# Second layer's first product with seven products for eight

## The chip, the cores and the metric

One core of a Trainium2 chip runs the whole program. The metric is the device time of one execution in microseconds (us); three runs of the kernel before gave 948.76, 949.13 and 949.52, median 949.13. A profile of one more execution is read below. Its engines are TensorE (PE, with its weight loads as PEld), VectorE (DVE), ScalarE (ACT), GpSimd (POOL) and SyncE (SP), which here only issues DMAs.

## The reference

Attention with random features over 4 batches, 8 heads, 576 tokens each (2304 tokens in all), then two layers over the 2304 x 512 result:

```
x = attention(q, k, v, omega)          # 2304 x 512
h = x @ moe_w_in                       # 512 -> 2048
x = (h * cos(h)) @ moe_w_out           # 2048 -> 512
h = x @ moe2_w_in
x = (h * clip(h + 3, 0, 6) / 6) @ moe2_w_out
```

Weights are float64, the output is float32.

## The kernel before

Everything lives transposed: features on the 128 partitions, tokens along the free dimension. `xx` is an SBUF tile of 4 x 2304 columns that holds the layer's input, later its output, as four feature chunks. To reach more than the precision of one fp32r matmul, every operand is split into a rounded part and the rest (`rnd`, L262, and `sub`, L270), and each product is three matmuls (`passes`, L741): high with high, low weight with high, high weight with low.

Each layer is cut into 16 hidden blocks of 128 (`f`) and into token blocks of 512 (the last one has 256). A slot (`slot`, L815) is one `f` on one token block: 12 matmuls of the first product (4 feature chunks x 3, L829) into one PSUM bank (`at` or `pt` in turn), the nonlinearity on ACT and DVE (`nonlinear`, L689), its split into `gh` and `gl`, and 12 matmuls of the second product (4 output chunks x 3, L851), which add up over all `f` in four PSUM banks (`kv0`, `kv1`, `h`, `h`). Layer one runs in two halves of eight `f`: the first half stores its sums in DRAM (`yy`), the second (blocks of mode "add", L551) loads them (`yp`) and writes `xx`. Layer two (mode "full", L553) takes all 16 `f` per token block, so that a bank pair for `h` alternates and a slot's second product follows some slots behind its first.

Weights arrive as raw 64-bit words. `weight` (L577) turns half an `f` (512 columns) into one fp32 tile `wt`: one ACT and four DVE instructions (L601 to L621), then a high part on ACT and a low part on DVE or POOL into `wh[f]` and `wl[f]`. Layer two's weights overwrite layer one's, `f` by `f`, as those get free.

The order on every engine is written out ahead. `Plan.add` (L88) registers each task with a due time, the engines that could do it with a cost on each, the tasks it comes after, and a ring of buffers that it takes a place from; `Plan.order` (L92) plays the plan through with these costs, always giving a free engine the ready task with the lowest due time, and the instructions are issued in the order that this gives. Rings (L48) have a fixed number of places, taken in rotation; each place is a tile of its own. All DMAs are issued from SP, in that order. The framework adds the waits from the data that instructions touch.

Of the kernel before, what the change touches and what calls it, by code (L numbers as in the profile page):

```python
# [32 lines left out]

N_LATE = 8
# [12 lines left out]
W_MD = 8.02  # L47
RINGS = {  # L48
    "xT": 4, "nat": 4, "v": 4, "sq": 4, "mx": 4, "P": 6, "qt": 3, "xn": 2, "kvs": 4, "rd": 4,
    "at": 2, "pt": 2, "h": 2, "kv0": 1, "kv1": 1, "ws": 3, "wt": 3, "mxh": 4, "mxl": 4, "wk": 3, "gh": 2, "gl": 2, "yp": 3,  # L50
}
Y_BANKS = ["kv0", "kv1", "h", "h"]
# [23 lines left out]
class Task:  # L76
    def __init__(self, name, seq, key, engs, fn, after, alloc, use, late):
        self.name, self.seq, self.key, self.engs, self.fn = name, seq, key, engs, fn
        self.after, self.alloc, self.use, self.late = after, alloc, use, late


class Plan:
# [5 lines left out]
    def add(self, name, key, engs, fn, after=(), alloc=None, use=(), late=False):  # L88
        assert name not in self.tasks, name
        self.tasks[name] = Task(name, len(self.tasks), key + BIAS.get(kind_of(name), 0.0), engs, fn, list(after), alloc, list(use), late)  # L90

    def order(self):  # L92
# [11 lines left out]
        for t in tasks.values():  # L104
            deps = set(t.after) | set(t.use)
# [8 lines left out]
        rings = {r: [] for r in RINGS}  # L114
# [12 lines left out]
        def can(t, now):  # L127
            if ready_at[t.name] > now:
                return ready_at[t.name]
            if t.alloc:  # L130
                q = rings[t.alloc]
                k = len(q) - RINGS[t.alloc]
                if k >= 0:
                    r = released.get(q[k])
                    if r is None:
                        return None
                    if r > now:
                        return r
            return 0.0

# [3 lines left out]
        while len(done) < len(tasks):  # L144
# [6 lines left out]
            while again:  # L151
                again = False
                for e in engines:
# [31 lines left out]
                    if t.alloc:  # L185
                        rings[t.alloc].append(t.name)
# [7 lines left out]
                    for n in out.get(t.name, ()):  # L194
                        need[n.name] -= 1
                        lat = LAT[e] + (0.1 if "t" in n.engs and e != "t" else 0.0)
# [11 lines left out]
def attention_moe_moe2_kernel(  # L208
# [17 lines left out]
    wp = ctx.enter_context(tc.tile_pool(name="wp", bufs=1))  # L226
    xp = ctx.enter_context(tc.tile_pool(name="xp", bufs=1))
    sb = ctx.enter_context(tc.tile_pool(name="sb", bufs=1))
    dp = ctx.enter_context(tc.tile_pool(name="dp", bufs=1, space=bass.MemoryType.DRAM))
    hps = ctx.enter_context(tc.tile_pool(name="hps", bufs=1, space=PSUM))  # L230
    actx = ExitStack()
    ap = actx.enter_context(tc.tile_pool(name="ap", bufs=1))
# [5 lines left out]
    def tile_of(pool, name, ring, shape, dt=F32):  # L238
        buf[name] = pool.tile(shape, dt, tag=ring, name=ring, bufs=RINGS[ring])
        return buf[name]  # L240

    def bank(name, ring):
        return tile_of(hps, name, ring, [128, 512])

    xx = xp.tile([128, KC, NT], F32, name="xx")
    yy = dp.tile([KC, 128, NT], F32, name="yy")
    wh, wl = {}, {}
    for f in range(NW):
        wh[f] = wp.tile([128, 1024], F32R, name=f"wh{f}")
        wl[f] = wp.tile([128, 1024], F32R, name=f"wl{f}")  # L250

    def open_late():
        actx.close()
        late_p = ctx.enter_context(tc.tile_pool(name="late_p", bufs=1, reuse_waits="tile"))
        for f in range(NW, NF):
            wh[f] = late_p.tile([128, 1024], F32R, name=f"wh{f}")
            wl[f] = late_p.tile([128, 1024], F32R, name=f"wl{f}")
# [16 lines left out]
    omd = ap.tile([128, M], F32, name="omd")  # L274
    ident = ap.tile([128, 128], F32, name="ident")
    zero = ap.tile([128, 256], F32, name="zero")
    half = ap.tile([128, M], F32, name="half")
    junk = ap.tile([128, 1], F32, name="junk")

    def warm(e):  # L280
        nc.vector.memset(zero, 0.0)
        p = bank("warm", "h")
# [28 lines left out]
    def chunk(kind, c, k, exp_after, lead, pr, prev, on_pe=False):  # L311
# [4 lines left out]
        def load(e):  # L316
            t = tile_of(ap, X, "xT", [128, 512])
# [5 lines left out]
        if not on_pe:  # L323
            add(A, k - lead + 0.5, {"d": 0.74},
                lambda e: nc.sync.dma_start(out=tile_of(ap, A, "nat", [128, 512]), in_=(kn if isk else qn)[c]), [("nat",) + prev] if prev else [], alloc="nat")
        if isk and c == 0:
            add("omr", k - lead + 0.01, {"d": 0.3}, lambda e: nc.sync.dma_start(out=omd, in_=omT))
        if isk:
            def load_v(e):
                nc.sync.dma_start(out=tile_of(ap, V, "v", [128, H * (D + 1)]), in_=vn[c])  # L330
# [3 lines left out]
        def square(e):  # L334
            a = tile_of(ap, A, "nat", [128, 512]) if on_pe else buf[A]
# [6 lines left out]
        def sums(e):  # L342
            sq = tile_of(ap, SQ, "sq", [128, 8])
# [17 lines left out]
        add(P0, k - 0.2, {"t": 0.01}, lambda e: bank(P0, pr), before, alloc=pr, use=[X])  # L361

        def proj(e):
            bank(("pj", kind, c, 1), pr)
# [22 lines left out]
        for hf in range(2):  # L387
            def tops(e, hf=hf):
                pj = buf["pj", kind, c, hf].rearrange("p (h m) -> p h m", h=4)
                if hf == 0:  # L390
                    tile_of(ap, MX, "mx", [128, 24])
# [18 lines left out]
        for hf in range(2):  # L410
            E = ("e", kind, c, hf)

            def exps(e, hf=hf, E=E):
                pj, mx = buf["pj", kind, c, hf], buf[MX]
                p = tile_of(ap, E, "P", [128, 512])
# [8 lines left out]
        if isk:  # L424
            for hf in range(2):
                E = ("e", kind, c, hf)
                for b, r0, r1 in rows(c):
                    def kv(e, b=b, r0=r0, r1=r1, hf=hf, E=E, first=not kv_parts[b, hf]):
                        if first:
                            bank(("kv", b, hf), f"kv{hf}")  # L430
# [16 lines left out]
                    if c == last_chunk[b] and b == rows(c)[0][0]:  # L447
                        def fin(e, b=b, hf=hf):
                            if hf == 0:
                                tile_of(ap, ("kvs", b, 0), "kvs", [128, 2, 260])  # L450
# [6 lines left out]
        for hf in range(2):  # L457
            E, TP, QT, NUM, RD = ("e", kind, c, hf), ("tp", c, hf), ("qt", c, hf), ("num", c, hf), ("rd", c, hf)

            def trq(e, E=E, TP=TP):  # L460
                p = bank(TP, "pt")
# [4 lines left out]
            def qt(e, TP=TP, QT=QT):  # L466
                rnd(e, tile_of(ap, QT, "qt", [128, 512]), buf[TP])
# [4 lines left out]
            def num(e, QT=QT, NUM=NUM, hf=hf):  # L472
                p = bank(NUM, "pt")
# [11 lines left out]
            def eps(e, NUM=NUM, RD=RD):  # L485
                rd = tile_of(ap, RD, "rd", [128, 8])
# [6 lines left out]
            def norm(e, NUM=NUM, RD=RD, hf=hf):  # L493
                p = buf[NUM][:, :260].rearrange("p (h d) -> p h d", h=4)
                rd = buf[RD]
                if hf == 0:
                    tile_of(ap, ("xn", c, 0), "xn", [128, H, D])
# [10 lines left out]
        def xtr(e):  # L508
            xn = buf["xn", c, 0]
            p = bank(("xt", c), "pt")  # L510
# [40 lines left out]
    blocks += [dict(m=1, t0=t0, n=n, fs=range(NW, NF), mode="add") for t0, n in whole]  # L551
    n_m1 = len(blocks)
    blocks += [dict(m=2, t0=t0, n=n, fs=range(NF), mode="full") for t0, n in whole]  # L553

    def last_use(f):
        return max(bi for bi in range(n_m1) if f in blocks[bi]["fs"])

# [18 lines left out]

    def weight(src, m, f, hf):  # L577
# [8 lines left out]
        elif f < NW:  # L586
            k = blocks[n_add]["t"] + 10.0 + 9.0 * j
        else:
            k = slots[where[n_m1, f]][2] - 30.0
        cols = slice(512 * hf, 512 * hf + 512)  # L590

        def load(e):
            t = tile_of(sb, ("ws",) + W, "ws", [128, 512, 2], U32)
            nc.sync.dma_start(out=t.rearrange("p c w -> p (c w)"), in_=src[f, :, 1024 * hf:1024 * hf + 1024])

        gate = W_GATE.get(j) if m == 1 else None
        add(("ws",) + W, k - 8, {"d": 1.5}, load, [last_w[0]] if last_w[0] else [], alloc="ws")

        def mag(e):
            w = tile_of(sb, ("wt",) + W, "wt", [128, 512])  # L600
            nc.scalar.activation(out=w, in_=buf[("ws",) + W][:, :, 1].bitcast(F32), func=ACTF.Abs)  # L601
# [11 lines left out]
        def sign(e):  # L613
            u = buf[("wt",) + W].bitcast(U32)
            nc.vector.scalar_tensor_tensor(
                out=u, in0=buf[("ws",) + W][:, :, 1], scalar=SIGN_HI, in1=u, op0=ALU.bitwise_and, op1=ALU.bitwise_or
            )

        def low(e):
            u = buf[("wt",) + W].bitcast(U32)  # L620
            nc.vector.scalar_tensor_tensor(  # L621
                out=u, in0=buf[("ws",) + W][:, :, 0], scalar=29, in1=u, op0=ALU.logical_shift_right, op1=ALU.bitwise_or
# [14 lines left out]
        if m == 2:  # L637
            g = slot_of(last_use(f), f)
            after += [("in", g, KC - 1)] if hf == 0 else [out_name(g, KC - 1)]

        add(("wh",) + W, k, {"a": 0.62}, lambda e: rnd(e, wh[f][:, cols], buf[T_]), after, use=[T_], late=late)
        add(("wl",) + W, k, {"p": 1.4} if m == 1 and f < WL_P else {"p": 1.4, "v": 0.72},
            lambda e: sub(e, wl[f][:, cols], buf[T_], wh[f][:, cols].bitcast(F32)), [("wh",) + W], use=[T_], late=late)
# [8 lines left out]
    for m, src in ((1, w1), (2, w2)):  # L652
        for f in range(NF):
            for hf in range(2):
                weight(src, m, f, hf)
# [3 lines left out]
    def x_split(bi, i):  # L659
# [18 lines left out]
        def hi(e):  # L678
            rnd(e, view(tile_of(sb, ("xh", bi, i), "mxh", [128, 512], F32R)), src())

        def lo(e):
            sub(e, view(tile_of(sb, ("xl", bi, i), "mxl", [128, 512], F32R)), src(), view(buf["xh", bi, i]).bitcast(F32))
# [6 lines left out]
    def nonlinear(g, m, k, n, IN, sn_after):  # L689
# [7 lines left out]
        if m == 1:  # L697

            def u1(e):
                nc.vector.tensor_scalar(  # L700
                    out=tile_of(sb, WK, "wk", [128, 512])[:, :n], in0=hb(), scalar1=0.25, scalar2=MAGIC, op0=ALU.add, op1=ALU.add
# [17 lines left out]
        else:  # L719
            def relu(e):  # L720
                nc.scalar.activation(  # L721
                    out=tile_of(sb, WK, "wk", [128, 512])[:, :n], in_=hb(), func=ACTF.Relu, bias=three
# [9 lines left out]
        def g_hi(e):  # L732
            rnd(e, tile_of(sb, GH, "gh", [128, 512], F32R)[:, :n], buf[WK][:, :n])

        def g_lo(e):
            sub(e, tile_of(sb, GL, "gl", [128, 512], F32R)[:, :n], buf[WK][:, :n], buf[GH][:, :n].bitcast(F32))
# [4 lines left out]
    def passes(f, xh, xl):  # L741
        return (wh[f], xh), (wl[f], xh), (wh[f], xl)

    def pair_slot(g):
# [5 lines left out]
        for q in range(4):  # L750
            def m_in(e, q=q):
                if q == 0:
                    bank(("h", g), "h")
# [16 lines left out]
                alloc=None if q else "h", use=[(x, bi, q % 2) for x in ("xh", "xl")] + ([("h", g)] if q else []))  # L770
# [4 lines left out]
        for ec in range(KC):  # L775
            def m_out(e, ec=ec):
                y2 = ec // 2
                if first and ec % 2 == 0:
                    bank(("y", bi, ec), Y_BANKS[y2])
# [16 lines left out]
                alloc=Y_BANKS[ec // 2] if al else None, use=[("gh", g), ("gl", g)] + ([] if al else [("y", bi, ec - ec % 2)]))  # L796
# [213 lines left out]
```

## Time and profile before

| What | us |
|---|---|
| median of 3 runs | 949.13 |
| span of the profiled execution (first to last instruction) | 947.4 |
| around the span (median less span) | 1.7 |
| TensorE busy in the span | 941.4 |
| VectorE busy | 581.1 |
| ScalarE busy | 441.2 |
| GpSimd busy | 89.9 |

The profiled execution's own time is not listed apart from its span; the runs agree within 0.8 us, so the median stands for it, and 1.7 us lie around the span. Attention and the first pieces of layer one fill the span to about 240 us, layer one goes on to about 555, and layer two's matmuls run from 544.9 to the end. A matmul's "busy" time includes its way through the array, which overlaps the next one; its cost is the distance from one start to the next.

### The profile page before, as it was taken

How to read it: one execution, taken by the hardware profiler on the slowest of the kernel's cores; microseconds unless marked ns; L12 is line 12 of the kernel's file. 1: busy time of each engine (PE TensorE's matmuls, PEld its weight loads, DVE VectorE, ACT ScalarE, POOL GpSimd, SP SyncE). 2: the span in 40 equal slices, each digit the busy share in tenths (PEclk: the TensorE clock that was granted, in tenths of full speed). 3: DMA queues.
4: the chain of work that ended last, by engine and by line, in shares of the span. 5: the costliest groups of instructions: out<-in, count | busy, mean ns of one | idle time of the engine just before them, and what ended most of it. 6: DMA issues, size and time to landing. Idle time of an engine off the chain costs nothing.

```text
span 947.4 us, 16225 instructions
## 1 busy us (share of the span) xinstructions
PE 941.4 (99%) x6582; PEld 817.0 (86%) x6582; DVE 581.1 (61%) x1095; ACT 441.2 (47%) x897; POOL 89.9 (9%) x86
## 2 busy tenths in 40 slices
PE   9999999999999999999999999999999999999998
PEld 8889899999888898888888988888888888888898
DVE  6899887555888998989474888442223223322322
ACT  6888887766444464533232544332224223322332
POOL 3444331111100000000000000000000000000000
PEclk9999999999999999999999999999999999999999
DMA  8776333100323233323110123001001000100010
GB/s 282 234 233 214 110 126 122 56 1 24 112 90 114 87 111 112 111 75 107 52 45 1 51 95 111 1 2 45 0 1 45 1 1 1 45 1 1 1 45 24
DMA packets 29963, 68.37 MB, mean 72 GB/s; under 512 B 3136, under 2 KB 7232, under 8 KB 29888
## 3 DMA queue, kind: packets, MB, share of 16 engines
q1 hardware_dynamic: 29888, 67.33, 21.7%
q8 instruction: 52, 0.85, 0.4%
q14 instruction: 23, 0.19, 0.1%
HBM read 57.88 MB, written 9.44 MB: 71 GB/s over the span
## 4 chain that ended last, share of the span: by engine, by line
PE 98%; ACT 1%; DVE 1%; issue 0%
PE at L829 19%; PE pt L829 19%; PE kv L851 18%; PE h L851 18%; PE kv L786 5%; PE h L760 5%; PE at L367 3%; PE kv L434 2%; PE pt L477 2%; PE pt L464 2%; PE h L367 1%; PE kv L927 1%; PE pt L512 1%; PE h L376 1%; PE at L376 1%; PE h L284 0%
## 5 line engine op out<-in xcount | busy, mean ns | idle before, releaser
L264 ACT ACTIVATE gh<-wk 128x512 fp32r<-128x512 f32 (+1 forms) x160 | 94.2, 589 | 117.1 <-DVE wk L727 39.4
L271 DVE TENSOR_TENSOR gl<-wk,gh 128x512 fp32r<-128x512 f32 (+1 forms) x144 | 92.3, 641 | 64.6 <-ACT gh L264 63.2
L829 PE MATMUL at<-mxh,wl 128*128 128x512 f32 (+1 forms) x288 | 105.3, 366 | 0.0
L829 PE MATMUL at<-mxh,wh 128*128 128x512 f32 (+1 forms) x288 | 105.3, 366 | 0.0
L851 PE MATMUL kv<-gh,wl 128*128 128x512 f32 (+1 forms) x288 | 105.3, 366 | 0.0
L829 PE MATMUL pt<-mxh,wl 128*128 128x512 f32 (+1 forms) x288 | 105.3, 366 | 0.0
L829 PE MATMUL pt<-mxh,wh 128*128 128x512 f32 (+1 forms) x288 | 105.3, 366 | 0.0
L851 PE MATMUL kv<-gh,wh 128*128 128x512 f32 (+1 forms) x288 | 105.3, 365 | 0.0
L829 PE MATMUL at<-mxl,wh 128*128 128x512 f32 (+1 forms) x288 | 105.2, 365 | 0.0
L829 PE MATMUL pt<-mxl,wh 128*128 128x512 f32 (+1 forms) x288 | 105.2, 365 | 0.0
L851 PE MATMUL h<-gh,wl 128*128 128x512 f32 (+1 forms) x288 | 105.2, 365 | 0.0
L851 PE MATMUL kv<-gl,wh 128*128 128x512 f32 (+1 forms) x288 | 105.2, 365 | 0.0
L851 PE MATMUL h<-gl,wh 128*128 128x512 f32 (+1 forms) x288 | 105.2, 365 | 0.0
L851 PE MATMUL h<-gh,wh 128*128 128x512 f32 (+1 forms) x288 | 105.2, 365 | 0.0
L710 ACT ACTIVATE wk<-wk,halfpi 128x512 f32<-128x512 f32 (+1 forms) x80 | 54.2, 679 | 91.8 <-DVE wk L706 91.7
L727 DVE SCALAR_TENSOR_TENSOR wk<-wk,at 128x512 f32<-128x512 f32 (+1 forms) x40 | 25.4, 634 | 96.7 <-ACT wk L721 96.7
L727 DVE SCALAR_TENSOR_TENSOR wk<-wk,pt 128x512 f32<-128x512 f32 (+1 forms) x40 | 25.4, 634 | 90.1 <-ACT wk L721 89.9
L721 ACT ACTIVATE wk<-at,three 128x512 f32<-128x512 f32 (+1 forms) x40 | 25.9, 647 | 104.5 <-PE at L829 104.5
L266 POOL TENSOR_SCALAR mxh<-xx 128x512 fp32r<-128x512 f32 (+1 forms) x20 | 16.2, 813 | 610.8 <-PE pt L829 337.3
L721 ACT ACTIVATE wk<-pt,three 128x512 f32<-128x512 f32 (+1 forms) x40 | 25.9, 647 | 92.1 <-PE pt L829 91.5
L851 PEld LDWEIGHTS kv<-gh,wh 128*128 128x128 f32 x288 | 54.3, 189 | 8.9
L851 PEld LDWEIGHTS h<-gh,wh 128*128 128x128 f32 x288 | 54.4, 189 | 8.9
(110 smaller groups left out, 2033.6 us busy)
## 6 DMA issues: line engine op xcount, KB each, us to landing
ws<-w SPq DMA_DIRECT2D x64, 512.0 KB, 3.8
v<-vn SPq DMA_DIRECT2D x18, 260.0 KB, 4.0
xT<-qT SPq DMA_DIRECT2D x18, 256.0 KB, 2.7
xT<-kT SPq DMA_DIRECT2D x17, 256.0 KB, 3.8
yy<-yp SPq DMA_DIRECT2D x16, 256.0 KB, 2.1
yp<-yy SPq DMA_DIRECT2D x16, 256.0 KB, 4.1
nat<-qn SPq DMA_DIRECT2D x15, 256.0 KB, 4.4
yT<-xx SPq DMA_DIRECT2D x9, 256.0 KB, 2.7
```

The costliest lines, as they stand in the source:

```text
L264: nc.scalar.activation(out=o, in_=i, func=ACTF.Copy)
L271: (nc.gpsimd if e == "p" else nc.vector).tensor_tensor(out=o, in0=a, in1=b, op=ALU.subtract)
L367: nc.tensor.matmul(out=buf["pj", kind, c, o][:, 128 * i:128 * i + 128], lhsT=buf[X][64 * o:64 * o + 64, 128 * i:128 * i + 128], rhs=omd[64 ...
L376: nc.tensor.matmul(out=buf["pj", kind, c, o][:, 128 * i:128 * i + 128], lhsT=buf[A][64 * o:64 * o + 64, 128 * i:128 * i + 128], rhs=half[6 ...
L434: nc.tensor.matmul(out=p[j:j + 64, 65 * h:65 * h + 65], lhsT=buf[E][r0:r1, 128 * h + j:128 * h + j + 64], rhs=buf[V][r0:r1, 65 * (2 * h + ...
L710: nc.scalar.activation(out=r, in_=r, func=ACTF.Sin, scale=-TURN, bias=halfpi)
L721: nc.scalar.activation(out=tile_of(sb, WK, "wk", [128, 512])[:, :n], in_=hb(), func=ACTF.Relu, bias=three)
L727: nc.vector.scalar_tensor_tensor(out=w, in0=w, scalar=6.0, in1=hb(), op0=ALU.min, op1=ALU.mult)
L760: nc.tensor.matmul(out=o, lhsT=w[:, 128 * kc:128 * kc + 128], rhs=v, start=(kc == 0 and j == 0), stop=(kc == KC - 1 and j == 2), skip_grou ...
L786: nc.tensor.matmul(out=y, lhsT=w[:, o], rhs=v, start=(first and fi == 0 and j == 0 and ec % 2 == 0), stop=(last and fi == 1 and j == 2 and ...
L829: nc.tensor.matmul(out=buf["h", g][:, :n], lhsT=w[:, 128 * kc:128 * kc + 128], rhs=x, start=(kc == 0 and j == 0), stop=(kc == KC - 1 and j ...
L851: nc.tensor.matmul(out=buf["y", bi, ec][:, :n], lhsT=w[:, o], rhs=x, start=(first and j == 0), stop=(last and j == 2),)
```

## The change

Layer two is rewritten; attention and layer one keep their instructions.

- **First product.** Hidden blocks are taken in pairs (`j`, 8 of them) and tokens in passes of 768 (`p`, 3 of them), each pass seen as two halves of 384 columns. For a pair and a pass (a "quad" in the code, 24 of them) the 2 x 2 product over (two hidden blocks) x (two feature pairs) x (two token halves) is made with seven products, Strassen's scheme in Winograd's form. Each product is 6 matmuls of 384 columns (2 feature chunks x 3). ACT copies a PSUM bank into another bank at three places, so that later products add to an earlier sum; one bank is copied to SBUF and added on DVE.
- **Forms.** The sums of weights that the seven products need (`pair_forms`) and the sums of tokens (`forms`, seven per pass, each 2 x 768 columns, high and low) are made on DVE, ACT and POOL. The token forms of a pass are written to DRAM (`xd`) when first made and loaded again on later visits.
- **Order.** Four sweeps of two pairs go over the three passes, back and forth: 12 steps of two quads. The second product of a step comes in 8 units (12 matmuls of 384 columns, over two pairs, in one of two PSUM banks); its result is added into `xx` by DVE (in the first sweep written by ACT or DVE).
- **Places.** SBUF is now four large tiles (`R1`, `R2`, `F1`, `F2`) and every ring is a list of column ranges in them; the planner picks the place that gets free first, and for the rings in `TURNS` the next in turn. PSUM is eight fixed bank tiles.
- **Layer one.** Its last five blocks come in the order 0, 4, 1, 2, 3, and the loads of `yp` may start two slots earlier.

The diff, cut to its core:

```diff
+T_P = 31.1
+NS = 384
+NP = 2 * NS
+SWEEP = 2
 RINGS = {
-    "xT": 4, ... "at": 2, "pt": 2, "h": 2, "kv0": 1, "kv1": 1, "ws": 3, "wt": 3, "mxh": 4, ...
+    **stacked(R1, 0, ("w0", 2048, NG)),
+    **stacked(R2, 0, ("w1", 2048, NF - NG)),
...
+    "hb": spread(PS, 0, 1, 4) + spread(PS, 6, 1, 2),
+    "yb": spread(PS, 4, 1, 2),
+    "wf": spread(R1, 0, 3584, 2) + spread(R2, 0, 3584, 1),
+    "wo": spread(R1, 7168, 2048, 2) + spread(R2, 3584, 2048, 1),
+    "xf": spread(R1, 11264, 1536, 3) + spread(R2, 5632, 1536, 5),
+    "g2": spread(R1, 16384, 768, 8) + spread(R2, 13312, 768, 4),
...
+    "ta": spread(F1, XX + 1024, 768, 2),
+    "hs": spread(F1, XX + 2560, 384, 1) + spread(F1, XX + 5632, 384, 2),
+    "wk2": spread(F1, XX + 6400, 384, 3),
 }
-    blocks += [dict(m=1, t0=t0, n=n, fs=range(NW, NF), mode="add") for t0, n in whole]
+    blocks += [dict(m=1, t0=t0, n=n, fs=range(NW, NF), mode="add") for t0, n in whole[:1] + whole[4:] + whole[1:4]]
-    blocks += [dict(m=2, t0=t0, n=n, fs=range(NF), mode="full") for t0, n in whole]
+    ORDER = [0, 4, 1, 5, 6, 2, 3]
+    WITH = [(0, "b11"), (1, "b21"), (6, "b22"), (2, "t4"), (3, "t1"), (4, "t2"), (5, "t3")]
...
+        def forms(s, p):
...
+            if s:
+                for i, x in enumerate(names):
+                    def load(e, X=X, i=i):
+                        nc.sync.dma_start(out=tile_of(X, [128, 2 * NP]).bitcast(F32), in_=xd[p, i])
...
+            sums = {"t1": ("b12", "b11"), "t3": ("b22", "b12"), "t2": ("b22", "t1"), "t4": ("b21", "t2")}
...
+                add(X, kk + 0.3, {"a": 0.78, "p": 1.3}, hi, after + gate, alloc="xf", use=use, soft=behind(names.index(x)))
+                add(("xfl", p, x), kk + 0.4, {"v": 0.88, "p": 1.9}, lo, [X], use=use + [X])
...
+            product(0, A, True, first, "hb")
+            seed(Bk, A, 1.1, [A])
+            product(4, E, True, [A], "hb")
...
+            c11 = product(1, A, False, [Bk, E])
+            u2 = product(5, Bk, False, [c11])
+            seed(C, Bk, 7.4, [u2])
+            u3 = product(6, Bk, False, [C, u2])
+            seed(Dk, Bk, 9.6, [u3])
+            c12 = product(2, C, False, [u3])
+            c21 = product(3, Dk, False, [c12])
...
+                add(WK, k + dk, {"a": 0.5}, relu, [done], alloc="wk2", use=[h])
+                add(("gg",) + G[1:], k + dk + 0.5, {"v": 0.48}, gg, use=[WK, h])
+                add(G, k + dk + 1.0, {"a": 0.45}, ghi, [("gg",) + G[1:]], alloc="g2", use=[WK])
+                add(("gl2",) + G[1:], k + dk + 1.5, {"v": 0.5}, glo, use=[WK, G])
...
+                        for i in range(SWEEP):
+                            for r in range(2):
+                                for a, v in ((h, g[:, 0:NS]), (l, g[:, 0:NS]), (h, g[:, NS:2 * NS])):
+                                    nc.tensor.matmul(out=o, lhsT=a, rhs=v, start=q == 0, stop=q == 6 * SWEEP - 1)
```

`seed(to, frm, ...)` is an ACT copy of 384 columns from bank `frm` into bank `to`.

## Rows read from the trace of the kernel before

**Rows 1.** The page, parts 1 and 2: busy us; GB/s in 40 slices.

```profile
PE 941.4 (99%) x6582; PEld 817.0 (86%) x6582; DVE 581.1 (61%) x1095; ACT 441.2 (47%) x897; POOL 89.9 (9%) x86
...
GB/s 282 234 233 214 110 126 122 56 1 24 112 90 114 87 111 112 111 75 107 52 45 1 51 95 111 1 2 45 0 1 45 1 1 1 45 1 1 1 45 24
```

**Rows 2.** The page, part 4: the chain that ended last, by engine.

```profile
PE 98%; ACT 1%; DVE 1%; issue 0%
```

**Rows 3.** Windows: stretch, length, busy PE PEld DVE ACT POOL, clock, DMA.

```profile
0.00:150.00 150.00, 147.94 (x2152) 133.72 (x2153) 128.88 (x267) 122.02 (x334) 57.45 (x56) 1.00 0.60 198
150.00:545.00 395.00, 394.75 (x2477) 344.73 (x2477) 304.52 (x583) 191.98 (x352) 27.35 (x26) 1.00 0.23 73
...
600.00:943.50 343.50, 343.50 (x1697) 292.29 (x1696) 101.88 (x163) 102.01 (x170) 3.75 (x4) 1.00 0.04 13
```

**Rows 4.** Chain by time, two stretches: start, us, what, how many.

```profile
414.79 2.72 PE at L829 x12
...
901.94 1.44 PE pt L829 x12
```

**Rows 5.** Groups by form, PE, from 545: count, busy us, mean ns, idle.

```profile
L829 PE MATMUL at<-mxh,wh 128*128 128x512 f32 x128 | 49.8, 389 | 0.0
...
L829 PE MATMUL pt<-mxh,wh 128*128 128x256 f32 x32 | 9.1, 283 | 0.0
```

**Rows 6.** Timeline, DVE, 541.8 to 543: start, us, engine, line, instruction.

```profile
541.87 0.42 DVE L271 TENSOR_TENSOR gl<-wk,gh 128x256 fp32r<-128x256 f32 x1
542.21 0.69 DVE L271 TENSOR_TENSOR mxl<-xx,mxh 128x512 fp32r<-128x512 f32 x1
542.81 0.42 DVE L700 TENSOR_SCALAR wk<-pt 128x256 f32<-128x256 f32 x1
```

**Rows 7.** Groups by form, DVE, from 545: weights.

```profile
L621 DVE SCALAR_TENSOR_TENSOR wt<-ws,wt 128x512 uint32<-128x512 uint32 x12 | 8.2, 688 | 0.2
...
L609 DVE TENSOR_SCALAR wt<-wt 128x512 uint32<-128x512 uint32 x12 | 5.0, 423 | 0.2
```

**Rows 8.** Groups by form, ACT, from 545.

```profile
L264 ACT ACTIVATE gh<-wk 128x512 fp32r<-128x512 f32 x64 | 40.4, 631 | 48.4 <-DVE wk L727 38.9 <-PE h L851 8.2 <-DVE wt L621 1.2
L721 ACT ACTIVATE wk<-pt,three 128x512 f32<-128x512 f32 x32 | 22.1, 690 | 84.8 <-PE pt L829 84.7
...
L264 ACT ACTIVATE gh<-wk 128x256 fp32r<-128x256 f32 x18 | 7.5, 416 | 13.4 <-PE h L851 12.8 <-DVE wk L727 0.5
...
L868 ACT ACTIVATE xx<-kv 128x512 f32<-128x512 f32 x8 | 4.8, 598 | 0.6 <-PE kv L851 0.2
...
L868 ACT ACTIVATE xx<-kv 128x256 f32<-128x256 f32 x2 | 0.7, 384 | 1.5 <-PE kv L851 1.5
```

**Rows 9.** Timeline, 658 to 661; idle before and releaser in brackets.

```profile
658.09 0.39 PE L851 MATMUL kv<-gh,wh 128*128 128x512 f32 x1
658.29 0.69 ACT L721 ACTIVATE wk<-at,three 128x512 f32<-128x512 f32 x1 [3.36 <-PE at L829]
...
659.01 0.69 DVE L727 SCALAR_TENSOR_TENSOR wk<-wk,at 128x512 f32<-128x512 f32 x1 [3.36 <-ACT wk L721]
...
659.73 0.63 ACT L264 ACTIVATE gh<-wk 128x512 fp32r<-128x512 f32 x1 [0.75 <-DVE wk L727]
...
660.40 0.69 DVE L271 TENSOR_TENSOR gl<-wk,gh 128x512 fp32r<-128x512 f32 x1 [0.70 <-ACT gh L264]
```

**Rows 10.** DMA issues of the page: KB each, us to landing.

```profile
ws<-w SPq DMA_DIRECT2D x64, 512.0 KB, 3.8
```

**Rows 11.** Timeline, PE, 942 to the end: the last matmul.

```profile
943.42 0.28 PE L851 MATMUL h<-gl,wh 128*128 128x256 f32 x1
```

**Rows 12.** Groups by form, DVE, 0 to 150: weights, token splits.

```profile
L621 DVE SCALAR_TENSOR_TENSOR wt<-ws,wt 128x512 uint32<-128x512 uint32 x17 | 14.6, 856 | 0.1
...
L609 DVE TENSOR_SCALAR wt<-wt 128x512 uint32<-128x512 uint32 x19 | 13.0, 688 | 0.1
...
L271 DVE TENSOR_TENSOR mxl<-xx,mxh 128x512 fp32r<-128x512 f32 x6 | 5.4, 896 | 0.0
```

More of the change, by code (lines that the diff above doesn't have):

```diff
@@ L86, in __init__, with add @@
         self.tasks = {}
-    def add(self, name, key, engs, fn, after=(), alloc=None, use=(), late=False):
+    def add(self, name, key, engs, fn, after=(), alloc=None, use=(), late=False, soft=()):
         assert name not in self.tasks, name
-        self.tasks[name] = Task(name, len(self.tasks), key + BIAS.get(kind_of(name), 0.0), engs, fn, list(after), alloc, list(use), late)
+        self.tasks[name] = Task(name, len(self.tasks), key + BIAS.get(kind_of(name), 0.0), engs, fn, list(after), alloc, list(use), late, list(soft))
     def order(self):
@@ L104, in order @@
         for t in tasks.values():
-            deps = set(t.after) | set(t.use)
+            deps = set(t.after) | set(t.use) | set(t.soft)
             need[t.name] = len(deps)
@@ L130, in can, with slots_of, free_at, take @@
             if t.alloc:
[L131 to L138, printed above, removed]
-            return 0.0
+                r = min(free_at(x) for x in slots_of(t.alloc))[0]
+                if r == NEVER:
+                    return None
+                if r > now:
+                    return r
+            return 0.0
+        def slots_of(ring):
+            r = RINGS[ring]
+            return r if ring not in TURNS else [r[taken.get(ring, 0) % len(r)]]
+        def free_at(x):
+            space, lo, hi = x
+            at = 0.0
+            for o, l, h in live.get(space, ()):
+                if l < hi and lo < h:
+                    at = max(at, released.get(o, NEVER))
+            return at, lo, x
+        def take(t):
+            space, lo, hi = x = min(free_at(x) for x in slots_of(t.alloc))[2]
+            taken[t.alloc] = taken.get(t.alloc, 0) + 1
+            live[space] = [(o, l, h) for o, l, h in live.get(space, ()) if l >= hi or lo >= h] + [(t.name, lo, hi)]
+            self.slot[t.name] = x
         for t in tasks.values():
@@ L360, in chunk @@
         before = [("pj",) + prev + (1,)] if prev else []
-        add(P0, k - 0.2, {"t": 0.01}, lambda e: bank(P0, pr), before, alloc=pr, use=[X])
+        add(P0, k - 0.2, {"t": 0.01}, lambda e: bank(P0), before, alloc=pr, use=[X])
         def proj(e):
-            bank(("pj", kind, c, 1), pr)
+            bank(("pj", kind, c, 1))
             for i in range(4):
@@ L637, in weight @@
         if m == 2:
[L638 to L643, printed above, removed]
+            return
+        add(("wh",) + W, k, {"a": 0.62}, lambda e: rnd(e, wh(f)[:, cols], buf[T_]), after, alloc=None if hf else "w0" if f < NG else "w1",
+            use=[T_] + ([("wh", m, f, 0)] if hf else []), late=late)
+        add(("wl",) + W, k, {"p": 1.4} if f < WL_P else {"p": 1.4, "v": 0.72},
+            lambda e: sub(e, wl(f)[:, cols], buf[T_], wh(f)[:, cols].bitcast(F32)), [("wh",) + W], use=[T_, ("wh", m, f, 0)], late=late)
     def slot_of(bi, f):
@@ L650, in out_name @@
         return ("out", g, ec) if f != blocks[bi]["fs"][0] else ("y", bi, ec)
[L652 to L655, printed above, removed]
+    t_2[0] = t
+    for f in range(NF):
+        for hf in range(2):
+            weight(w1, 1, f, hf)
+    for j in range(NF // 2):
+        for hf in range(2):
+            for f in (2 * j, 2 * j + 1):
+                weight(w2, 2, f, hf)
     last_x = [None]
@@ L721, in relu @@
                 nc.scalar.activation(
-                    out=tile_of(sb, WK, "wk", [128, 512])[:, :n], in_=hb(), func=ACTF.Relu, bias=three
+                    out=tile_of(WK, [128, 512])[:, :n], in_=hb(), func=ACTF.Relu, bias=three
                 )
@@ L934, in filler @@
         if ("fill", ring) not in buf:
-            bank(("fill", ring), ring)
+            buf["fill", ring] = banks[RINGS[ring][0][1]]
         return lambda: nc.tensor.matmul(out=buf["fill", ring][:, 0:FILL], lhsT=zero[:, 0:128], rhs=zero[:, 0:FILL], start=True, stop=True)
```

409 lines of the change are left out of this document (335 added, 74 removed).

## The prediction

> **What bounds the kernel now.** I read the page first: TensorE is busy 941.4 of 947.4 us [rows 1], and the chain that ended last is 98% TensorE with nothing in "issue" [rows 2]. That figure alone is weak, because a matmul's busy time overlaps the next one's, so I went on to the windows [rows 3]: from 600 to 943.5 us, inside layer two, TensorE has no idle time at all, at full granted clock, while VectorE is busy 102 of 343.5 us, ScalarE 102 and GpSimd 4. Layer two is therefore bound by the number of matmuls times their spacing, and the other engines have two thirds of their time to give away. The chain by time gives the spacing [rows 4]: twelve matmuls of 512 columns take 2.72 us, 226.7 ns each; twelve of 256 columns take 1.44 us, 120.0 ns each. (The mean of 389 ns in the groups [rows 5] is latency; what is used from there is the count: 12 groups of 128, 1536 matmuls of 512 columns, and for the 256-token block 12 groups of 32, 384.)
>
> **What the change removes.** Before, layer two costs 1536 x 226.7 ns = 348.2 us and 384 x 120.0 ns = 46.1 us: 394.3 us. After, the first product has 24 quads x 7 products x 6 = 1008 matmuls of 384 columns instead of 1152 such, and the second 96 units x 12 = 1152, unchanged in columns. The trace holds no 384-column matmul. From both sides: 0.75 of the 512 price is 170.0 ns, 1.5 times the 256 price is 180.0 ns; midway between the two measured points on a line it is 173.3 ns, which I take, since both points lie about 13 ns above columns/2.4 GHz. Sum after: 2160 x 173.3 = 374.4 us. **Saved: 19.9 us** (ends 27.1 and 5.5). Weight loads change at every matmul in both versions and hide at 256 columns already.
>
> **What it adds beside TensorE.** Spacing on VectorE is 0.34 us for 256 columns and 0.60 for 512 [rows 6], so 0.47 for 384, 0.86 for 768, 1.12 for 1024. Per quad: two additions of banks, four `gg`, four low parts, 10 x 0.47 = 4.7 us, times 24 = 113. Additions into `xx` in sweeps two to four: 72 x 0.47 = 34. Token forms: 3 passes x (7 low parts + 4 sums) x 0.86 = 28. Weights: 32 halves x (2 x 0.42 + 2 x 0.69 = 2.2, [rows 7]) = 71, and per pair 2.1 for low parts of the forms, 1.4 for sums, 1.2 for the second weights, x 8 = 37. Together 283 us for 374 us of matmuls, 76%; some 37 us of it (two pairs, one pass) come before layer two starts. In the first sweep alone: 6 quads 28, two passes of forms 19, two pairs 27: 74 of 93 us. ScalarE: a bank copy of 384 is (598 + 384)/2 = 0.49 us, a rounding 0.52, a relu 0.58 (by the same slope) [rows 8]; 12 such per quad, 6.3 x 24 = 151, plus weights and forms of about 77: 228 of 374. Both fit beside TensorE; all of this costs nothing while it keeps its order, and shows as waits when it does not.
>
> **What it puts on the path.** Before, TensorE never waits in layer two because a bank's way to the next product takes 3.0 us (658.09 to 661.09, [rows 9]) and other slots' matmuls cover it. Now there are places with less cover.
> - *Bank copies.* The product `u3` needs bank C, which ScalarE copies after `u2`; what releases what in the timeline is 0.20 us from the last matmul to ScalarE [rows 9], 0.49 for the copy and some 0.06 back: 0.75 us. The first and third copy have a product of 6 x 0.173 = 1.04 us beside them; the second has nothing of its own quad and needs a unit (2.08 us) or a product of the next quad in between. The planner picks any ready task on TensorE, and in steps 2 to 12 units of the previous step are there: four per quad for one gap. Queued behind a copy on ScalarE are relus and roundings, and those hold banks. I take 2 us in all for copies that come late because ScalarE was in another instruction; ends 0 and 34 (second rival).
> - *The first step* has no units: the second quad's first products fill part of two bare gaps, 1.5 us (0 to 3).
> - *Token forms of passes two and three* can be made only as places of `xf` (eight for seven forms) get free, product by product. From the second quad of a step to the end of the next quad's products are 14.6 us of matmuls or more; VectorE needs 11 x 0.86 + 4.7 = 14.2 us in them. That only just fits: 2 us for both (0 to 10). Later visits load them from DRAM: 768 KB each, at most 7 in a 31 us step, 5.5 MB or 177 GB/s; the page shows slices at 282 GB/s [rows 1] and 512 KB landing in 3.8 us [rows 10], 5.7 us in proportion, against the 15 us between a place's release and its use. SP, which issues them, stands at each load until the product has released the place, and weight loads queue behind; they are due tens of us later. Cost 0 (0 to 6, in the range only).
> - *Seams of sweeps.* `wo` has three places for pairs; the second pair of a sweep gets its place when the last unit of the sweep before is through, two roundings and two low parts before the next unit. Products go on meanwhile: 1 us for three seams (0 to 6).
> - *The end.* The last units need the last product's relu, `gg`, rounding and low part: 0.20 + 0.58 + 0.56 + 0.52 + 0.56 + 0.1 = 2.5 us, with at most one unit of 2.08 before them: 1.5 us (0.4 to 2.5). From the last matmul (943.42, [rows 11]) to the end of the span are 4.0 us, a copy and a store; after it is an addition and a store, 0.
>
> Attention and layer one keep their instructions; the placement frees buffers by the same uses, and the reorder of five blocks moves nothing between engines: 0 (-2 to +2), since TensorE idles 2.3 us before 545 us in all [rows 3].
>
> **The sum.** 947.4 - 19.9 + (2 + 1.5 + 2 + 1 + 1.5 = 8.0) = 935.5 us of span. The profiled span lies 1.7 us under the median of the runs shown; with that, 937.2 us.
>
> **Rivals.**
> 1. *GpSimd slows VectorE.* The planner may give sums and low parts to GpSimd. In the first 150 us GpSimd is busy 57 us [rows 3], and there the same VectorE instructions take 856 instead of 688 ns, 688 instead of 423 [rows 7, 12], token splits 896 [rows 12] instead of 690 [rows 6]: 1.24 to 1.63 times. At 1.3 times, the first sweep's 74 us become 96, over the 93 of TensorE, and each later low part may come late: about 10 us more, 947 us. Against it: GpSimd needs twice VectorE's time by the planner's costs, so it gets a task only while VectorE is within a long one. The Trainium skill (SBUF — State Buffer, "Who interferes with whom") says that VectorE and GpSimd share a port pair as an exclusive lock: a VectorE instruction with two SBUF inputs, or in a two-port mode, blocks against a GpSimd instruction that reads SBUF, for its whole length. The trace agrees (the 1.24 to 1.63 above); by the rule the token sums would be the worst partners of GpSimd's low parts, and by it the time would be the 947 us just given.
> 2. *Bare bank copies (slower).* If no unit stands at the gap, because units were spent earlier in the step or their `g2` are late, each quad pays 0.75 us for the second copy, and each of three copies queues behind a ScalarE instruction (61% busy, half of 0.5 us left: 0.15, more behind one that itself waits, up to 0.6). With 0.75 + 0.65 per quad, 24 x 1.4 = 33.6 us: 947.4 - 19.9 + 33.6 + 6 + 1.7 = 969 us. It decides from 0.6 us per quad on, where 24 x 0.6 and the other 6 us have used up the saving. For it: seven products in a chain, six banks for five sums per quad. Against it: the plan puts any ready matmul in a gap, and the plan before kept TensorE idle for 2.3 us in 545.
> 3. *The saving is smaller than the count says.* If a 384-column matmul costs one and a half of the 256, 388.8 us remain: 947.4 - 5.5 + 8 + 1.7 = 951.6 us. For it only that the form is not in the trace; against it that the two prices differ by 13 ns of fixed cost.
> 4. *All gaps filled.* With 1.5 us at the end and 1 elsewhere: 947.4 - 19.9 + 2.5 + 1.7 = 931.7, down to 929 where the matmul costs 172 ns.
>
> **How the numbers follow.** Forecast 0.64, its own range 933 to 945; rival 1 0.11, rival 2 0.14, rival 3 0.03, rival 4 0.08. A measurement here can tell 0.2% (1.9 us) from no change: faster is below 947.2, slower above 951.0. The forecast and rival 4 are faster, rival 1 to two thirds, rival 2 is slower but for its lower edge; faster 0.79, same 0.07, slower 0.14. The range of 8 in 10 leaves out most of rival 2 and a little at the bottom: 929 to 950.
>
> **What would show it.** 384-column matmuls 173 ns apart; a step of 31.2 us of matmuls, and layer two's TensorE idle under 10 us, in pieces at the first two steps, the seams and the last 3 us before the final units. Wrong if TensorE waits on ScalarE's bank copies once per quad (rival 2), on VectorE's low parts with GpSimd busy (rival 1), or on loads of `xf`.

## The result: 937.84 us, where 937.2 was forecast

The changed kernel takes 937.84 us (median of 4 runs, 937.08 to 937.95); the kernel before took 949.06 beside it. The ratio is 0.9879, with a 95% interval of 0.9865 to 0.9892: faster, by 11.2 us. The number came out; the split behind it did not. Layer two gained more than forecast, and layer one lost time for which the forecast had no term.

The page of the changed kernel, part 1, answers to [rows 1] (busy us, share, instructions), and the windows answer to [rows 3] (stretch, length, busy PE PEld DVE ACT POOL, clock, DMA share, GB/s):

```profile
PE 928.4 (99%) x6822; PEld 857.9 (92%) x6822; DVE 681.2 (73%) x1295; ACT 500.8 (54%) x1048; POOL 88.8 (9%) x81
```

```profile
0.00:150.00 150.00, 147.42 (x2146) 133.21 (x2147) 128.83 (x264) 120.63 (x331) 60.12 (x56) 1.00 0.62 198
150.00:545.00 395.00, 394.75 (x2482) 341.65 (x2482) 288.61 (x541) 184.70 (x337) 22.72 (x21) 1.00 0.20 65
...
600.00:931.00 331.00, 331.00 (x1900) 331.00 (x1899) 215.26 (x413) 158.31 (x311) 5.94 (x4) 1.00 0.43 151
```

TensorE is as full as before. In the third line 1900 matmuls of 384 columns take 331 us, 174.2 ns each, with no idle time, though the busy share of VectorE is 2.2 times and that of ScalarE 1.6 times that of [rows 3]. Every wait of TensorE from 545 us to the end (engine, line, what it waited for: us in all, times, longest):

```profile
PE b L1186 <- DVE F L1220: 0.4, 1, 0.4
PE b L1186 <- ACT b L1198: 0.2, 1, 0.2
PE b L1186 <- DVE F L1238: 0.2, 1, 0.2
```

The first matmuls around each wait are further apart as well (283 to 287 ns for 174). Together the distances hold 1.9 us over their usual spacing in all of layer two, all of it before 577 us, in the first step. The end has no wait either: the last three matmuls follow at their usual distance. From the last one to the end of the span are 4.2 us, where it was 4.0 before [rows 11] (timeline: start, us, engine, line, instruction).

```profile
931.38 0.68 PE L1272 MATMUL b<-R 128*128 128x384 f32 x3
...
932.10 0.56 DVE L1289 SCALAR_TENSOR_TENSOR F<-b,F 128x384 f32<-128x384 f32 x1 [1.55 <-PE b L1272]
```

Layer two gained 16.0 us (17.9 of matmuls less 1.9 of waits, see the account below), but the span is only 11.4 us shorter. The chain by time (start, us, what, how many) shows where most of the rest went: into layer one, whose instructions are those of before. The last two lines are layer two's 384 columns.

```profile
302.59 2.72 PE b L939 x12
...
430.55 2.80 PE b L917 x12
433.35 2.80 PE b L939 x12
...
749.92 1.06 PE b L1186 x6
750.98 2.11 PE b L1272 x12
```

Twelve matmuls of 512 columns take 2.72 us in layer one's first half, as before it at 414.79 us [rows 4], and 2.80 in its second half. VectorE and ScalarE are less busy there than in [rows 3] (second line of each), and TensorE does not wait.

**The account of the span**, 947.4 to 936.0. Layer two's matmuls: 394.3 to 376.4 (2160 x 174.3), -17.9. Layer two's idle time: +1.9. Attention, until layer one's first slot: 238.96 to 239.66, +0.7. Layer one from there, with its last second products that run among layer two's first (36 of 256 columns before, 24 of 512 after): 544.88 + 4.3 - 238.96 = 310.2 before, 547.99 + 5.6 - 239.66 = 313.9 after, +3.7. Behind the last matmul: +0.2. Sum -11.4.

### The profile page after: what moved, and what is told of

It is laid out like the page before. It is cut to its first block, busy times and chain, and to the rows that moved or that the text cites. A ratio compares the mean times of both kernels' runs of the same rounds, so it can differ in the third digit from the quotient of the medians.

```text
span 936.0 us, 17221 instructions
## 1 busy us (share of the span) xinstructions
PE 928.4 (99%) x6822; PEld 857.9 (92%) x6822; DVE 681.2 (73%) x1295; ACT 500.8 (54%) x1048; POOL 88.8 (9%) x81
## 4 chain that ended last, share of the span: by engine, by line
PE 97%; ACT 1%; DMA 1%; DVE 1%; issue 0%; SPq 0%; ACTq 0%
PE b L1272 21%; PE b L1186 18%; PE b L917 17%; PE b L939 17%; PE b L874 5%; PE b L848 5%; PE b L446 4%; PE b L513 3%; PE b L556 2%; PE b L543 2%; PE b L455 2%; PE b L1323 1%; PE b L591 1%; DMA F<-kT 1%; ACT R L343 0%
## 5 line engine op out<-in xcount | busy, mean ns | idle before, releaser
L343 ACT ACTIVATE R<-F 128x512 fp32r<-128x512 f32 (+4 forms) x297 | 171.6, 599 | 113.8 <-DVE F L801 33.1
L350 DVE TENSOR_TENSOR R<-F,R 128x512 fp32r<-128x512 f32 (+4 forms) x273 | 179.3, 673 | 38.5 <-ACT R L343 32.5
L1272 PE MATMUL b<-R 128*128 128x384 f32 x684 | 141.4, 336 | 0.0
L1272 PEld LDWEIGHTS b<-R 128*128 128x128 f32 x684 | 120.9, 188 | 0.0
L1186 PE MATMUL b<-R,R 128*128 128x384 f32 x564 | 109.5, 336 | 0.7 <-DVE F L1220 0.4
L917 PE MATMUL b<-R,R 128*128 128x512 f32 (+1 forms) x480 | 106.5, 372 | 0.0
L939 PE MATMUL b<-R,R 128*128 128x512 f32 (+1 forms) x480 | 106.2, 372 | 0.0
L798 ACT ACTIVATE F<-F,halfpi 128x512 f32<-128x512 f32 (+1 forms) x80 | 54.3, 680 | 96.9 <-DVE F L794 96.8
L1272 PE MATMUL b<-R,R 128*128 128x384 f32 x468 | 102.3, 336 | 0.0
L1186 PEld LDWEIGHTS b<-R,R 128*128 128x128 f32 x564 | 98.6, 188 | 1.8 <-ACT b L1198 0.9
L939 PEld LDWEIGHTS b<-R,R 128*128 128x128 f32 x480 | 83.8, 188 | 17.4
L917 PEld LDWEIGHTS b<-R,R 128*128 128x128 f32 x480 | 82.8, 188 | 16.7
L350 POOL TENSOR_TENSOR R<-F,R 128x512 fp32r<-128x512 f32 (+1 forms) x36 | 47.6, 1322 | 494.0 <-ACT R L343 491.8
L1186 PE MATMUL b<-R 128*128 128x384 f32 x444 | 87.3, 337 | 0.2 <-DVE F L1238 0.2
L498 ACT ACTIVATE F<-b,F 128x128 f32<-128x128 f32 x288 | 81.1, 392 | 8.6 <-DVE F L483 6.3
L1272 PEld LDWEIGHTS b<-R,R 128*128 128x128 f32 x468 | 83.3, 188 | 0.0
L788 DVE TENSOR_SCALAR F<-b 128x512 f32<-128x512 f32 (+1 forms) x80 | 50.9, 636 | 43.5 <-PE b L917 26.7
L1186 PEld LDWEIGHTS b<-R 128*128 128x128 f32 x444 | 78.4, 188 | 0.6 <-DVE F L1238 0.5
L801 DVE TENSOR_TENSOR F<-b,F 128x512 f32<-128x512 f32 (+1 forms) x80 | 50.6, 633 | 21.1 <-ACT F L798 21.0
```

The costliest lines, as they stand in the source:

```text
L343: nc.scalar.activation(out=o, in_=i, func=ACTF.Copy)
L350: (nc.gpsimd if e == "p" else nc.vector).tensor_tensor(out=o, in0=a, in1=b, op=ALU.subtract)
L498: nc.scalar.activation(out=p[:, o], in_=pj[:, o], func=ACTF.Exp, scale=-1.0, bias=mx[:, b:b + 1])
L788: nc.vector.tensor_scalar(out=tile_of(WK, [128, 512])[:, :n], in0=hb(), scalar1=0.25, scalar2=MAGIC, op0=ALU.add, op1=ALU.add)
L798: nc.scalar.activation(out=r, in_=r, func=ACTF.Sin, scale=-TURN, bias=halfpi)
L801: nc.vector.tensor_tensor(out=buf[WK][:, :n], in0=hb(), in1=buf[WK][:, :n], op=ALU.mult)
```

## The experiments

**What differs in layer one's second half.** Its weights (`f` 8 to 15) are now in `R2`, which by the sizes of the tiles ahead of it starts 64 bytes further on modulo 128 than `R1`, where its tokens are. Before, all operands started at 64 modulo 128. My theory was placement: the spacing of matmuls depends on where weights and moving operand start relative to each other. The rivals were the new order of the last five blocks, and load from VectorE, ScalarE or DMA. Sorted by that phase, the 512-column matmuls of the changed kernel are 226.9 ns apart with equal phases and 233.3 with different ones; the 256-column ones 119.8 and 113.4.

*a1: only layer one's late weights move.*

```diff
-SIZES = {R1: 22528, R2: 16384, F1: 18112, F2: 16384}
+SIZES = {R1: 22528, R2: 16400, F1: 18096, F2: 16384}
-    "wf": spread(R1, 0, 3584, 2) + spread(R2, 0, 3584, 1),
+    "wf": spread(R1, 0, 3584, 2) + spread(R2, 16, 3584, 1),
...
```

(`wo`, `xf` and `g2` in `R2` 16 words further on as well, so that layer two stays where it was.)

> Layer one's weights of f 8 to 15 move 64 bytes down (from 64 to 0 modulo 128, where its tokens already are); layer two's tiles keep the class they had. Placement theory: the 768 matmuls of 512 columns of layer one's second half go from 233.3 to 226.9 ns (-4.9 us), the 192 of 256 columns from 113.4 to 119.8 (+1.2): time 934.1 us, 3.7 below the changed kernel. Rivals (the order of the last blocks, VectorE, ScalarE or DMA load beside them): no change, 937.8.

Measured: 934.93 us (5 runs, ratio to before 0.985, 0.9837 to 0.9863). The same place of the chain:

```profile
431.17 2.72 PE b L917 x12
433.89 2.72 PE b L939 x12
```

By the account above, layer one is 545.24 + 5.4 - 240.36 = 310.3 us, that of the kernel before. Placement carries the loss; the order of the blocks and the load were left as they were. The time fell by 2.9 us and not by 3.6, since in this profile attention ends 0.7 us later (240.36 for 239.66).

*a2: all of R2 moves.* `SIZES` has F1 at 18096 and nothing else changes.

> All of R2 moves 64 bytes down, so every matmul operand of the kernel starts at 0 modulo 128. Placement theory: layer one as in the run before (-3.7); layer two's products all at the 177.3 ns that this class showed instead of 175.9 on the mean (+1.4), units 174.5 for 174.4: 935.6 us. If the classes matter only at 512 and 256 columns: 934.1. Rivals without placement: 937.8.

Measured: 932.84 us (5 runs, 0.9828, 0.9816 to 0.9841), the fastest kernel here. Layer one is 310.3 us as in a1, and layer two gained too, against what I had read from the changed kernel's means by phase. From 600 us on:

```profile
600.00:928.00 328.00, 328.00 (x1894) 328.00 (x1893) 213.93 (x410) 157.12 (x309) 5.94 (x4) 1.00 0.42 151
```

That is 173.2 ns each, and all are 173 or 174 apart, where the changed kernel's lie between 168 and 185. A mean by the phase of one matmul misled me; a likely reason, not shown, is that in a mixed sequence the spacing belongs to the neighbours as much as to the matmul. From the first product to the end of the span: 386.0 us, 388.0 in the changed kernel.

*a3: the kernel before, with its late weights moved.*

```diff
+        late_p.tile([128, 16], F32, name="pad")
         for f in range(NW, NF):
             wh[f] = late_p.tile([128, 1024], F32R, name=f"wh{f}")
```

> The kernel before, with a pad of 64 bytes ahead of the weights of f 8 to 15 in both layers: these go from 64 to 0 modulo 128, tokens stay at 64. Placement theory: 1536 matmuls of 512 columns from 226.8 to 233.3 ns (+10.0), 384 of 256 columns from 119.9 to 113.4 (-2.5): 956.5 us, 7.5 above the kernel before. Rival (the changed kernel's order or load made its layer one longer): 949.1, no change.

Measured: 957.8 us (4 runs, 1.009, 1.0075 to 1.0104). The loss appears in the kernel before, with its order and its load:

```profile
441.54 1.40 PE kv L852 x6
442.94 1.40 PE h L852 x6
444.34 2.80 PE pt L830 x12
```

Six would be 1.36 us, half of the twelve of [rows 4]. Layer one is 314.1 us by the account, +3.9, and the rest is layer two's. The 512-column matmuls with different phases are 233.4 ns apart, the 256-column ones 115.7, not 113.4; hence 8.4 us and not 7.5.

*a4: layer two's weights at 64, its moving operands at 0 modulo 128.* Same edits as a1 with 16 and 32 words, and F1 at 18064, which brings `R2` to 0 modulo 256 while `R1` is at 128.

> Layer one with all operands at 0 modulo 128 (-3.7), layer two with all weights at 64 and all moving operands at 0. By the means of the changed kernel's classes: products 173.9 for 175.9 ns (1008: -2.0 us), units 175.4 for 174.4 (1152: +1.2): 933.3 us. If classes do nothing at 384 columns: 934.1. Rivals without placement: 937.8.

Measured: 939.92 us (4 runs, 0.9895, 0.9879 to 0.9911). A miss, and the most useful one: equal phases modulo 128 are not enough. Layer one's late weights and its tokens are now 128 bytes apart modulo 256, and those matmuls are 232.4 ns apart; in a1 and a2, where the two are 256 bytes apart modulo 512, they are 227 apart. The period is 256 bytes. By the account layer one is 314.3 us, 4.0 longer than in a1, which makes up most of the miss of 6.6 us; part of the rest is attention, which ends at 241.92 us in this profile.

*m1: TensorE alone.*

```
t = one SBUF tile; 8 phases of weights x 8 of the moving operand x (512, 384, 256 columns),
18 matmuls each: (h, xh), (l, xh), (h, xl) ..., nothing else running
```

> Nothing of the reference is computed: TensorE alone runs the sequence (high, high), (low, high), (high, low) at 512, 384 and 256 columns, with the start of the weights and of the moving operand each at the eight multiples of 32 bytes within 256; no other engine works beside it. Placement theory: with both at one phase 226.9, 173.3 and 119.9 ns; 64 bytes apart about 233 at 512 columns, 113 to 116 at 256, 173 to 177 at 384. Rival (the spacing came from what ran beside in the kernels): 226.9, 173.3 and 119.9 for every pair of phases.

Measured: one run of 624.46 us, with VectorE, ScalarE and GpSimd idle and DMA at rest in the stretch (windows):

```profile
100.00:200.00 100.00, 100.00 (x432) 80.81 (x431) 0.00 (x0) 0.00 (x0) 1.00 0.00 0
```

The median distance by phase of the moving operand less that of the weights, from the records of the trace (within each 18, without the first three distances):

```
bytes      0    32    64    96   128   160   192   224
512 cols 227.0 234.0 229.0 232.0 231.5 234.0 233.0 232.0
384 cols 173.0 173.0 173.0 176.0 175.0 173.0 174.0 174.0
256 cols 120.0 118.0 118.0 119.5 119.0 117.0 117.0 117.0
```

At 512 columns the effect is TensorE's own: the eight pairs of phases with the same difference modulo 256 lie within 1.4 ns of each other (means; the first group of the run left aside), which bears out the period. At 256 the change of sign is there, but the medians show only 3 ns of the 6.4 of the changed kernel. Its 113.4 ns (moving operand 64 bytes behind the weights, 192 in the table) appears in two of the eight pairs of that column, where the distances settle at 113 to 114 ns; the other six average 117.7. So at 256 columns the difference alone does not decide; what else does is open.

**What fills the gaps of the first product.** The next three kernels start from a2, whose even spacing lets a few us be read.

*b1: eight products for seven.*

```diff
-                    for kc in range(2):
+                    for kc in (0, 1, 0, 1) if i == 3 else (0, 1):
...
```

> On the kernel with all operands at one phase (932.84 us), the seventh product of each quad is made twice, so that eight are paid for (its bank holds a wrong sum). If layer two is the count of matmuls times their spacing: 24 x 6 x 173.3 ns = +25.0 us, 957.8 us. If waits in the chain of products set a part of the end, the extra matmuls fill them and the rise is smaller: with the 8 us of idle time of the forecast, +17, 949.8.

Measured: 955.38 us (4 runs, 1.0066, 1.005 to 1.0081), 22.5 over a2. Layer two by the profiles is 23.2 longer: 25.0 of matmuls, less some 1.7 of the first step's waits, which the extra product covers (its waits from 545 us on come to nothing that the view lists). The saving is the count of matmuls; without it, the second layer's new form is slower than the old (955.38 us, where the kernel before took 949.88 beside it).

*b2: units only between quads.*

```diff
+            m = n // 2
+            for t, u in ((m - 1, 3),) if n % 2 else ((m - 2, 7),):
+                if t >= 0:
+                    first = first + [("y2",) + tour[t] + (u,)]
...
+                        + [("sp", n0 + SWEEP + c, 3)]
```

> On the same kernel, the units of the second product run only between quads (four after each quad of the next step), so that no unit can stand at the second bank copy of a quad. Second rival of the forecast: 22 quads that had units x 0.75 us = +16.5, 949.3 us; with copies that queue behind other ScalarE work 1.4 each, +31, 963.6. If other matmuls than units cover the copies: 932.8 to 934.

Measured: 953.01 us (5 runs, 1.0041, 1.0027 to 1.0055), 20.2 over a2, slower than the kernel before. The waits from 545 us on, and one such place in the timeline:

```profile
PE b L1186 <- ACT b L1198: 14.8, 23, 1.0
```

```profile
834.38 0.86 PE L1186 MATMUL b<-R,R 128*128 128x384 f32 x4
...
834.99 0.66 ACT L686 ACTIVATE F<-F 128x512 f32<-128x512 f32 x1
835.55 0.48 ACT L1198 ACTIVATE b<-b 128x384 f32<-128x384 f32 x1
...
836.09 0.96 PE L1186 MATMUL b<-R,R 128*128 128x384 f32 x4 [0.85 <-ACT b L1198]
```

One copy per quad is bare. Of the 23, 16 cost 0.73 us at the next matmul and 0.10 in the one behind it; five cost 1.0 to 1.1 us at the next matmul, among them the place shown, where ScalarE was still in another instruction (L686). In the changed kernel the same copy lies beside a unit:

```profile
749.76 1.22 PE L1186 MATMUL b<-R,R 128*128 128x384 f32 x6
...
750.82 0.69 PE L1272 MATMUL b<-R,R 128*128 128x384 f32 x3
...
751.02 0.47 ACT L1198 ACTIVATE b<-b 128x384 f32<-128x384 f32 x1 [1.44 <-PE b L1186]
...
751.35 1.74 PE L1272 MATMUL b<-R 128*128 128x384 f32 x9
...
752.93 1.22 PE L1186 MATMUL b<-R 128*128 128x384 f32 x6
```

The product that the copy waits for is followed by the unit at 750.82, the copy ends at 751.49, and the product that needs it starts at 752.93, behind a unit (12 matmuls of L1272). By the order on TensorE at least one unit stands there in each of the last 21 quads, and a product of the next quad in the first three, ahead of the first units.

*c1: GpSimd beside layer two.*

```diff
+                    z = held((R1, 15872, 16384), [128, 512])
+                    sub("p", z, z.bitcast(F32), z.bitcast(F32))
...
+                add(("gp", m, i), start(m) + 2 * i, {"p": 1.75}, load, [("ba", m)] + ...)
```

> The kernel with all operands at one phase (932.84 us), and beside layer two eight GpSimd subtractions of 512 columns per quad (192 in all, on words that nothing else uses, about 1.7 us each, so that GpSimd is busy nearly throughout). First rival of the forecast: VectorE's instructions last 1.24 to 1.63 times as long; in the first sweep VectorE is busy 80.5 of 93 us, at 1.3 times 105, so TensorE waits about 12 us there, and the time is 943 to 945. If VectorE's spare time takes it: 933 to 935.

Measured: 1015.76 us (4 runs, 1.0696, 1.0679 to 1.0712), 82.9 over a2: a miss by far. Layer one took 13.6 us of it and layer two 69.2. GpSimd waits for nothing in these and ran ahead: 53 of 192 fell into layer one, the rest filled 545 to 735 us, at 1.3 us each. The window there, and VectorE's groups in it (count, busy us, mean ns, idle):

```profile
545.00:735.00 190.00, 141.29 (x653) 131.26 (x652) 177.40 (x166) 78.58 (x148) 179.19 (x139) 0.85 0.29 107
```

```profile
L350 DVE TENSOR_TENSOR R<-F,R 128x384 fp32r<-128x384 f32 x28 | 33.7, 1227 | 0.6 <-ACT R L343 0.6
...
L1238 DVE SCALAR_TENSOR_TENSOR F<-F 128x384 f32<-128x384 f32 x14 | 16.8, 1218 | 0.0
...
L1238 DVE SCALAR_TENSOR_TENSOR F<-F,b 128x384 f32<-128x384 f32 x14 | 7.6, 541 | 0.0
```

The changed kernel in the stretch from 548 to 735 us:

```profile
L350 DVE TENSOR_TENSOR R<-F,R 128x384 fp32r<-128x384 f32 x49 | 27.2, 575 | 2.4 <-ACT R L343 2.1
L1238 DVE SCALAR_TENSOR_TENSOR F<-F,b 128x384 f32<-128x384 f32 x25 | 13.8, 550 | 6.6 <-ACT F L1235 6.3
...
L1238 DVE SCALAR_TENSOR_TENSOR F<-F 128x384 f32<-128x384 f32 x24 | 13.2, 556 | 1.6 <-ACT F L1235 1.5
```

Factors of 2.1 and 2.2 for the forms with both inputs in SBUF, VectorE full, TensorE waiting 49 of 190 us at a mean granted clock of 0.85. The form of L1238 with one input in PSUM (`b`) kept its time: 541 ns for 550. TensorE's largest waits end at ScalarE's bank copies (27.8 us in 7), whose engine in turn waits for VectorE (most for L706, 24.9 us in 5):

```profile
PE b L1186 <- ACT b L1198: 27.8, 7, 7.2
```

That is the rule of the Trainium skill that the prediction named (SBUF — State Buffer, "Who interferes with whom"): only an instruction with two SBUF inputs, or in a two-port mode, is blocked. The trace shows the first half; that `TENSOR_SCALAR` of 512 columns with its one input in SBUF (L690) also went from 423 to 1094 ns would fit the second, but in which mode it ran is not shown.

*b3: layer one's last blocks back in order.*

```diff
-    ... for t0, n in whole[:1] + whole[4:] + whole[1:4]]
+    ... for t0, n in whole]
```

> The same kernel with layer one's last five blocks back in the order 0 to 4. If the order was a part of what layer one's second half lost or gained: a change of 0.5 us or more. If placement was all of it: layer one unchanged and the time 932.8, unless layer two's first step waits for the tokens of pass one (its products then start on blocks that were finished last): up to +3.

Measured: 946.81 us (10 runs, 942.99 to 948.96; 0.9966, 0.9952 to 0.998), 14.0 over a2 and more than either expectation. In this order part of the output is wrong, and why was not looked into; so the time is not that of a working kernel, and only waits and spacing are read here. From 545 to 600 us:

```profile
PE b L1186 <- DVE F L801: 4.8, 1, 4.8
PE b L1186 <- DVE F L1238: 2.8, 1, 2.8
```

```profile
554.37 0.42 DVE L801 TENSOR_TENSOR F<-b,F 128x256 f32<-128x256 f32 x1
...
554.84 1.97 PE L1186 MATMUL b<-R 128*128 128x384 f32 x5 [4.75 <-DVE F L801]
```

The expectation looked for a wait for tokens, and that is not what happened: layer one's last block is then the short one of 256 columns (tokens 2048 to 2303), and layer two's first pass needs the tokens up to 767, which lie in the first two of the five blocks. L801 is layer one's own nonlinearity, the last to read a PSUM bank that the product takes over, and VectorE is late with it: from 547 to 554 us it is mostly in token forms (L350 and L1150, 768 columns each). From 555 to 560 us, behind the wait, the granted clock is 0.50, the lower of the two levels, and 384-column matmuls are 320 ns apart for some 6 us, and for 3 us behind the second wait. Layer one's second half shows two more waits of 2.6 us in all (L917 for L801) and its 512-column matmuls otherwise at the distance of a2 (226.9 ns), so the order is no part of the 3.7 us. It seems to be what keeps the seam to layer two cheap, where the forecast put it at nothing; how much it is worth in a kernel with a right result is not shown.

## Why the prediction was right, and where its steps were not

- **What bounds the kernel**: right. Layer two is the count of matmuls times their spacing, before and after; b1 shows it by adding one product.
- **The matmul's price**: forecast 173.3 ns, measured 174.3, so 17.9 us saved and not 19.9. The 173.3, midway between the two prices of [rows 4], is right to a tenth where all operands have one phase, as in the kernel before (a2 and b1, from 600 us on). The 1.0 ns is placement. Rival 3 (180.0) is out.
- **Idle time of layer two**: forecast 8.0 us, measured 1.9, all of it the first step (forecast 1.5). The one late bank copy that the view lists (0.2 us, forecast 2) is part of that 1.9; token forms of passes two and three, seams and end cost nothing for 2, 1 and 1.5. Here the sum was mis-sized: I charged each place with a part of its worst case, though the planner had units to put there and TensorE waited for VectorE (262 of 387 us busy from 548 on; forecast 283 with what lay ahead of layer two) only in the first step.
- **Reloads of token forms**: cost 0 as forecast. 42 of 768 KB land in 6.1 us in the median (5.7 by proportion), and no wait names them.
- **Attention and layer one**: forecast 0 (-2 to +2), measured +4.4, outside its bounds. "The placement frees buffers by the same uses" looked at when buffers come free and not at where they start. Layer one's 3.7 us is that; a1 gives 3.6 back. That weight loads "hide at 256 columns already" was read from a kernel whose operands all had one phase; at 512 columns the place of the weights has a price (233.3 for 226.9 ns). The 0.7 us in attention lies within what profiles of kernels with the same attention show (the first slot starts between 237.7 and 242.0 us); what moves it is open.
- **Rival 4** (all gaps filled, 931.7), with a chance of 0.08, was the better picture of layer two. Where placement costs nothing (a2, 932.84) the time is 1.1 us from it.
- **Rival 2** had mechanism and price: 0.75 us forecast, 0.73 + 0.10 measured in b2, with the place named. It did not occur, since the plan puts other matmuls, in most quads a unit, at each gap.
- **Rival 1** did not occur: GpSimd has 4 instructions in layer two (5.9 us). Its price for the little work it assumed on GpSimd was not tested; with GpSimd busy throughout, c1 shows tens of us, VectorE's factors at 2.1 to 2.2 and not 1.3, and a granted clock of 0.85 on the mean beside TensorE's waits.

So the forecast hit by luck, by errors that cancel: idle time 6.1 us less, against matmuls 2.0 us, layer one with attention 4.4 and the end 0.2 more. The range (929 to 950) was wide enough for either alone.

## What to carry to other kernels

When buffers are placed by hand, look at the phase modulo 256 bytes of everything that TensorE reads. For fp32r matmuls of 512 and 384 columns, each with its own weight load, one phase for all was best here: 64 bytes less in one tile were worth 5.0 us of 937.8. At 256 columns different phases were faster. When an unchanged stage changes its time, compare the spacing of like matmuls in the chain first; it tells waiting from wider spacing in one row. Before charging a chain of short dependent steps with its gaps, count the independent matmuls that the plan can put there, and their number per gap.

## What the runs showed of the hardware that was not expected

The distance between fp32r matmuls of 512 columns is 226.9 ns when weights and moving operand start at one phase modulo 256 bytes, and 231 to 234 at nearly all others (64 bytes: 229), also with every other engine idle (m1). At 256 columns it is the other way round (119.9, and 113.4 to 120), at 384 nearly level (173.3, and 173 to 176). What in TensorE makes the difference is open. The Trainium skill (SBUF — State Buffer, "Who interferes with whom") gives TensorE two independent read ports, one for the moving operand and one for weight loads, and says that TensorE never waits on anyone. No other engine is needed for the loss here, which agrees with the second; the dependence on the relative start of the two operands speaks against reading "independent" as free of each other, and there the measurement decides.
